# Reordering the TensorE and ScalarE program of a windowed-attention and feed-forward kernel, with a silu built from exp and ln

## The chip, the core and the metric

The kernel runs on one core of a Trainium2 chip. The metric is the device time of one execution in microseconds (us); the figure quoted for a kernel is the median of its runs. Lower is better.

## The reference, cut to what matters

The input is `x`, 2048 tokens of 448 features in bf16. It is normalised once (`xn`, no learned scale), and two branches read `xn`:

```python
# branch A: 16 heads of 28; each token looks at itself and at 7 earlier tokens, every second one
qkv = xn @ wqkv                        # 448 -> 3*448
logits = einsum(q, k[pos - 2*w]) * 28**-0.5     # w = 0..7, masked where pos - 2*w < 0
o = softmax(logits) . v[pos - 2*w]
s = o @ wo                             # 448 -> 448
# branch B: feed-forward
h = gelu(xn @ w1 + b1)                 # 448 -> 1792, tanh approximation
y = h @ w2 + b2                        # 1792 -> 448
g = silu(y)
return x + s * g
```

## The kernel before, in words

The tokens are loaded with the even ones first and the odd ones behind them, so that "every second token" becomes "the token before" and the window is 8 neighbours. They are held as 16 tiles of 128 tokens (index `t`) and as 4 chunks of 512 tokens (index `c`). `xnT` is the normalised input with features on the partitions.

**Jobs.** `qk_job(c, g, which)` makes q or k of one group of four heads for a chunk: 4 matmuls, and a cast by VectorE out of PSUM. `v_job(b)` makes v for one block of 128 keys: 4 matmuls, and a copy by ScalarE. `ffn1_pair(c, m0)` makes two of the 14 slices of the hidden layer: 8 matmuls, then two gelu activations on ScalarE into `hT`. `ffn2_job(t)` makes `y` of one tile: 14 matmuls and an addition by VectorE. `silu_job(t)` makes `g`, as twice silu: one Tanh on ScalarE, one VectorE operation. `wo_job(t)` makes the output of one tile: 4 matmuls, two VectorE operations (`sg` and `o_t`) and a store from SP's queue.

**Units.** Attention is done in 17 units: for chunk `c` and head group `i`, four blocks of 121 queries against 128 keys each; the last block (16) of all four groups is unit 4 of chunk 3. `qk_unit` makes the scores (16 matmuls into two PSUM buffers of pool `psA`), two Exp activations on ScalarE (`E`), and two VectorE multiplications of `E` by a mask. `av_unit` then makes the sums `psD` (4 matmuls) and the products `psO` (16 matmuls), Ln and Exp(-x) on ScalarE for the reciprocal (`ld`, `R`), and a VectorE multiplication into `oT`.

**PSUM.** Pool `psA` has two buffers, shared by `ffn1_pair` and by the two score tiles of a unit: the first scores behind a feed-forward stage need both buffers, and so the last gelu. Pool `psB` has four buffers, shared by all the rest.

**Tables.** Gelu and Tanh are in one table set of ScalarE, Exp and Ln in another; `preload_act_table_set` puts the change between them into the program.

**Order.** PE and ScalarE run in the order in which the program writes their instructions (`manual_schedule`). The instructions of VectorE, GpSimd and SP are ordered by the framework's planner. For every chunk `c` the program runs a stage of seven `ffn1_pair(c, ...)`, between them the silu of the chunk before, the normalisation and transposition (`ln_apply`, `ln_tr`) of the chunk after, and the `wo_job`s that are complete by then; then four units of chunk `c`, each as scores, one `ffn2_job`, up to three projections of the next chunk, `av_unit`. Chunk 3 has five units and no projections left to put between them. After the last unit come a change of table set, four silus and the last five `wo_job`s.

Of the kernel before, what the change touches and what calls it, by code (L numbers as in the profile page):

```python
# [8 lines left out]
F32 = mybir.dt.float32  # L9
BF16 = mybir.dt.bfloat16  # L10
U32 = mybir.dt.uint32
ALU = mybir.AluOpType
ACT = mybir.ActivationFunctionType
ENG = mybir.EngineType

S, D, H, DH, F = 2048, 448, 16, 28, 1792
P = 128
NT = S // P
NC = 4
# [4 lines left out]
QB = 121  # L24
# [9 lines left out]
def kernel(  # L34
# [14 lines left out]
    nc = tc.nc  # L49
# [4 lines left out]
    def dram_rows(par, t0, n):  # L54
        cls, r = divmod(t0 * P, S // 2)
        return par[cls, r:r + n * P, :].rearrange("(t p) d -> p t d", p=P)
# [3 lines left out]
    work = ctx.enter_context(tc.tile_pool(name="work", bufs=2))  # L60
# [11 lines left out]
    y_sb = [big.tile([P, D], F32, name=f"y_{i}") for i in range(4)]  # L72
    g_sb = [big.tile([P, D], BF16, name=f"g_{i}") for i in range(8)]
# [18 lines left out]
    def xt(t):  # L92
        return x_sb[t // 4][:, t % 4, :]
# [55 lines left out]
    def ln_stats(t):  # L149
        st = work.tile([P, 6], F32, name="st", tag="st", bufs=4)  # L150
        nc.vector.bn_stats(out=st[:], in_=xt(t))  # L151
        nc.vector.bn_aggr(out=mv[:, t, :], in_=st[:])

    def ln_rstd(t0, n):
        nc.scalar.activation(lnv[:, t0:t0 + n], mv[:, t0:t0 + n, 1], ACT.Ln, bias=eps_t[:])
        nc.scalar.activation(rstd[:, t0:t0 + n], lnv[:, t0:t0 + n], ACT.Exp, scale=-0.5)  # L156

    def ln_apply(t):
        nc.vector.tensor_scalar(xnb[t % 4][:, 0:D], xt(t), mv[:, t, 0:1], rstd[:, t:t + 1],  # L159
                                op0=ALU.subtract, op1=ALU.mult)  # L160

    def ln_tr(t):
        pT = psB.tile([P, KT, P], BF16, name="pT", tag="B")
        for kt in range(KT):
            nc.tensor.transpose(pT[:, kt, :], xnb[t % 4][:, kt * P:(kt + 1) * P], ident[:])  # L165
        nc.vector.tensor_copy(xnT[:, :, LEAD + t * P:LEAD + (t + 1) * P], pT[:, :, :])  # L166

    def qk_weights(kt):

        src = wqkv[:, kt, 0:32]  # L170
        nc.vector.tensor_copy(wqk[:, kt, :, :],
                              bass.AP(src.tensor, src.offset, [list(src.ap[0]), [DH, 2 * H], [1, 32]]))

    def qk_job(c, g, which):
        ps = psB.tile([P, CH], F32, name="ps_qk", tag="B")
        for kt in range(KT):
            nc.tensor.matmul(ps[:, :], wqk[:, kt, 16 * which + 4 * g:16 * which + 4 * g + 4, :],  # L177
                             xnT[:, kt, LEAD + c * CH:LEAD + (c + 1) * CH],
                             start=(kt == 0), stop=(kt == KT - 1))
        dst = (qT, kT)[which]  # L180
        nc.vector.tensor_copy(dst[:, g, LEAD + c * CH:LEAD + (c + 1) * CH], ps[:, :])  # L181

    def v_job(b):
        ps = psB.tile([P, D], F32, name="ps_v", tag="B")
        o = LEAD + QB * b - 7
        for kt in range(KT):
            nc.tensor.matmul(ps[:, :], xnT[:, kt, o:o + P], wqkv[:, kt, 2 * D:3 * D],  # L187
                             start=(kt == 0), stop=(kt == KT - 1))
        nc.scalar.copy(vw[b][:, :, 0:DH], ps[:, :].rearrange("p (h c) -> p h c", h=H))  # L189

    def ffn1_pair(c, m0):
        ps = psA.tile([P, 2, CH], F32, name="ps_h", tag="A")
        for i in range(2):
            m = m0 + i
            for kt in range(KT):
                nc.tensor.matmul(ps[:, i, :], w1[:, kt, m * P:(m + 1) * P],  # L196
                                 xnT[:, kt, LEAD + c * CH:LEAD + (c + 1) * CH],
                                 start=(kt == 0), stop=(kt == KT - 1))
        for i in range(2):
            m = m0 + i  # L200
            nc.scalar.activation(hT[0][:, m, :], ps[:, i, :], ACT.Gelu_apprx_tanh, bias=b1f[:, m:m + 1])  # L201

    def ffn2_job(t):
        c, tt = divmod(t, 4)
        ps = psB.tile([P, D], F32, name="ps_y", tag="B")
        for m in range(MT):
            nc.tensor.matmul(ps[:, :], hT[0][:, m, tt * P:(tt + 1) * P], w2[:, m, :],  # L207
                             start=(m == 0), stop=(m == MT - 1))
        nc.vector.tensor_tensor(out=y_sb[t % 4][:], in0=ps[:, :], in1=b2bc[:], op=ALU.add)

    def silu_job(t):
        th = work.tile([P, D], BF16, name="th", tag="th", bufs=2)
        nc.scalar.activation(th[:], y_sb[t % 4][:], ACT.Tanh, scale=0.5)  # L213
        nc.vector.scalar_tensor_tensor(out=g_sb[t % 8][:], in0=th[:], scalar=1.0, in1=y_sb[t % 4][:],  # L214
                                       op0=ALU.add, op1=ALU.mult)

    def wo_job(t):
        ps = psB.tile([P, D], F32, name="ps_s", tag="B")
        for g in range(4):
            nc.tensor.matmul(ps[:, :], oT[:, g, t * P:(t + 1) * P], wo[:, g, :],  # L220
                             start=(g == 0), stop=(g == 3))
        sg = work.tile([P, D], BF16, name="sg", tag="sg", bufs=2)
        nc.vector.scalar_tensor_tensor(out=sg[:], in0=ps[:, :], scalar=0.5, in1=g_sb[t % 8][:],  # L223
                                       op0=ALU.mult, op1=ALU.mult)
        o_t = work.tile([P, D], BF16, name="o_t", tag="o_t", bufs=3)
        nc.vector.tensor_tensor(out=o_t[:], in0=xt(t), in1=sg[:], op=ALU.add)
        nc.sync.dma_start(dram_rows(out_par, t, 1)[:, 0, :], o_t[:])
# [45 lines left out]

    SET_EXP, SET_GELU = "natural_log_exp_and_others", "gelu_apprx_tanh_and_others"

    def qkv_jobs(c):
        for g in range(4):
            for which in range(2):
                yield lambda g=g, which=which: qk_job(c, g, which)
        for b in range(4 * c, 4 * c + 4 + (c == 3)):  # L280
            yield lambda b=b: v_job(b)

    def run(it, n):
        for _ in range(n):
            f = next(it, None)
            if f is None:
                return
            f()


    with tc.manual_schedule(engines={ENG.PE, ENG.Activation}):
        nc.scalar.preload_act_table_set(SET_EXP)
        for t in range(4):
            ln_stats(t)
            ln_rstd(t, 1)
            ln_apply(t)
            ln_tr(t)
        for kt in range(KT):
            qk_weights(kt)
        for t in range(4, 8):  # L300
            ln_stats(t)
        ln_rstd(4, 4)
        run(qkv_jobs(0), 99)
        wo_next = 0
        for c in range(NC):

            nc.scalar.preload_act_table_set(SET_GELU)
            done = min(NT, 4 * QB * c // P)
            silu = iter(range(4 * (c - 1), 4 * c)) if c else iter(())
            for k in range(MT // 2):  # L310
                ffn1_pair(c, 2 * k)
                t = next(silu, None)
                if t is not None:
                    silu_job(t)
                if c + 1 < NC and k < 4:
                    ln_apply(4 * (c + 1) + k)
                    ln_tr(4 * (c + 1) + k)
                if k >= 2 and wo_next < done:
                    wo_job(wo_next)
                    wo_next += 1  # L320

            nc.scalar.preload_act_table_set(SET_EXP)
            if c + 2 < NC:
                for t in range(4 * (c + 2), 4 * (c + 3)):
                    ln_stats(t)
                ln_rstd(4 * (c + 2), 4)
            jobs = iter(list(qkv_jobs(c + 1))) if c + 1 < NC else iter(())
            n_units = 4 + (c == 3)
            for i in range(n_units):
                E = qk_unit(c, i)  # L330
                if i < 4:
                    ffn2_job(4 * c + i)
                run(jobs, 3 if i < 3 else 99)
                if i == 4:
                    pass
                av_unit(c, i, E)
        nc.scalar.preload_act_table_set(SET_GELU)
        for t in range(12, 16):
            silu_job(t)
        while wo_next < NT:  # L340
            wo_job(wo_next)
            wo_next += 1


# [1 line left out]
_INS = ['A_x', 'A_wqkv', 'A_wo', 'B_x', 'B_w1', 'B_b1', 'B_w2', 'B_b2']  # L346
# [26 lines left out]
```

## Time and profile before

| what | before |
|---|---|
| median of 3 runs | 201.92 us (201.13 to 202.17) |
| the profiled execution's own time | 203.14 us |
| its span, first to last instruction | 201.3 us |
| mean granted TensorE clock | 0.986 |
| TensorE (PE) busy | 172.6 us, 86% of the span |
| ScalarE (ACT) busy | 117.3 us, 58% |
| VectorE (DVE) busy | 111.8 us, 56% |
| chain that ended last, by engine | PE 73%, ACT 11%, DMA 6%, DVE 6%, issue 2% |

The profiled execution took 203.14 us, of which 201.3 us lie between its first and last instruction. PE's matmuls are pipelined, so the busy time of one contains some of its neighbour's; the chain of work that ended last shows the pace at which they follow one another. Granted clock 1.00 is 2.4 GHz.

### The profile page before, as it was taken

Reading aid. Unit: us, or ns where it says so; the run is one execution under the profiler, and the core shown is the slowest. Engines: PE = TensorE matmul, PEld = TensorE weight load, DVE = VectorE, ACT = ScalarE, POOL = GpSimd, SP = SyncE. Lnnn points to the kernel's source line nnn. Section 1 sums busy time; section 2 is a strip of 40 time slices with the busy share of each in tenths; the row PEclk is TensorE's granted clock in tenths of the full one; section 3 lists DMA queues with packets and bytes.
Section 4 is the critical chain, followed back from the end, with each engine's and each line's share of the span. In section 5 each row is a group of like instructions: output and inputs, shape, how many; then the busy total and the mean of one; then the engine's idle time right before and its main releaser. Section 6 shows DMA issues by size and latency. Waiting matters only on the chain.

```text
span 201.3 us, 3396 instructions
## 1 busy us (share of the span) xinstructions
PE 172.6 (86%) x1384; PEld 84.1 (42%) x1384; DVE 111.8 (56%) x220; ACT 117.3 (58%) x181; POOL 16.0 (8%) x56
## 2 busy tenths in 40 slices
PE   0048999979999999799999998899999997998570
PEld 0032445434455454345454543454444443444230
DVE  1886794009775356087753464377651651665494
ACT  0600057684356895745567965754469857657750
POOL 8966000000000000000000000000000000000000
PEclk9999999999999999999999999999999999999787
DMA  5999900000000001000000002000000010000002
GB/s 186 359 229 276 295 2 3 0 0 0 3 0 3 2 0 46 26 0 0 3 0 3 0 23 68 0 5 0 3 0 0 23 49 23 0 3 2 3 23 91
DMA packets 9743, 8.82 MB, mean 44 GB/s; under 512 B 2592, under 2 KB 8832, under 8 KB 9728
## 3 DMA queue, kind: packets, MB, share of 16 engines
q1 hardware_dynamic: 8704, 7.00, 12.4%
q10 hardware_dynamic: 512, 1.20, 1.6%
q0 software_dynamic: 512, 0.40, 1.0%
q8 instruction: 11, 0.18, 0.4%
q14 instruction: 4, 0.03, 0.0%
HBM read 6.77 MB, written 1.84 MB: 43 GB/s over the span
## 4 chain that ended last, share of the span: by engine, by line
PE 73%; ACT 11%; DMA 6%; DVE 6%; issue 2%; DVEq 0%
PE ps_h L196 23%; PE ps_y L207 16%; PE ps_qk L177 15%; PE ps_v L187 6%; DMA wqkv<-in_A_wqkv_dram 6%; PE ps_s L220 5%; ACT E L246 5%; ACT hT L201 3%; PE psD L257 3%; PE S L242 2%; DVE E L248 2%; PE psO L261 2%; ACT ld L266 1%; PE pT L165 1%; DVE sg L223 1%
## 5 line engine op out<-in xcount | busy, mean ns | idle before, releaser
L196 PE MATMUL ps_h<-xnT,w 128*128 128x512 bf16 x224 | 52.3, 379 | 0.2 <-ACT hT L201 0.2
L207 PE MATMUL ps_y<-w,hT 128*128 128x448 bf16 x224 | 45.2, 353 | 0.0
L201 ACT ACTIVATE hT<-ps_h,b1f 128x512 bf16<-128x512 f32 x56 | 35.4, 684 | 15.6 <-PE ps_h L196 15.5
L177 PE MATMUL ps_qk<-xnT,wqk 128*128 128x512 bf16 x128 | 32.1, 406 | 1.9 <-DVE xnT L166 1.9
L246 ACT ACTIVATE E<-S 128x976 bf16<-128x976 f32 x34 | 31.3, 973 | 0.0
L196 PEld LDWEIGHTS <-w 128*128 128x128 bf16 x224 | 21.3, 98 | 23.9 <-issue 0.5
L207 PEld LDWEIGHTS <-hT 128*128 128x128 bf16 x224 | 20.6, 98 | 19.2
L272 DVE TENSOR_TENSOR oT<-psO,R 128x484 bf16<-128x484 f32 (+1 forms) x17 | 11.2, 659 | 26.4 <-ACT R L267 26.4
L266 ACT ACTIVATE ld<-psD 128x484 f32<-128x484 f32 (+1 forms) x17 | 9.8, 574 | 24.0 <-PE psD L257 24.0
L189 ACT CAST vw<-ps_v 128x448 bf16<-128x448 f32 x17 | 9.0, 532 | 23.0 <-PE ps_v L187 23.0
L177 PEld LDWEIGHTS <-wqk 128*128 128x128 bf16 x128 | 13.1, 103 | 18.7 <-issue 3.8
L165 PE MATMUL pT<-ident,xnb 128*128 128x128 bf16 x64 | 6.7, 242 | 12.0 <-DVE xnb L159 12.0
L248 DVE TENSOR_TENSOR E<-E,mk_gen 128x976 bf16<-128x976 bf16 x18 | 12.0, 669 | 7.4 <-ACT E L246 7.4
L220 PE MATMUL ps_s<-wo,oT 128*128 128x448 bf16 x64 | 15.3, 376 | 0.0
L214 DVE SCALAR_TENSOR_TENSOR g<-th,y 128x448 bf16<-128x448 bf16 x16 | 9.8, 624 | 8.8 <-ACT th L213 8.7
L248 DVE TENSOR_TENSOR E<-E,mk 128x976 bf16<-128x976 bf16 x16 | 10.7, 668 | 7.0 <-ACT E L246 6.8
L187 PE MATMUL ps_v<-wqkv,xnT 128*128 128x448 bf16 x68 | 14.0, 352 | 0.0
L223 DVE SCALAR_TENSOR_TENSOR sg<-ps_s,g 128x448 bf16<-128x448 f32 x16 | 9.9, 622 | 7.0 <-PE ps_s L220 7.0
L159 DVE TENSOR_SCALAR xnb<-x,mv,rstd 128x448 bf16<-128x448 bf16 x16 | 5.7, 389 | 13.5 <-ACT rstd L156 13.5
L181 DVE CAST qT<-ps_qk 128x512 bf16<-128x512 f32 x16 | 11.0, 687 | 2.7 <-PE ps_qk L177 2.7
L181 DVE CAST kT<-ps_qk 128x512 bf16<-128x512 f32 x16 | 11.0, 689 | 2.1 <-PE ps_qk L177 2.0
L151 DVE BATCH_NORM_STATS2 st<-x 128x6 f32<-128x448 bf16 x16 | 9.5, 606 | 4.2 <-DMA x<-in_A_x_dram 4.2
(49 smaller groups left out, 136.2 us busy)
## 6 DMA issues: line engine op xcount, KB each, us to landing
out_dram<-o_t SPq DMA_DIRECT2D x16, 112.0 KB, 1.7
w<-in_B_w_dram SPq DMA_DIRECT2D x1, 1568.0 KB, 15.8
x<-in_A_x_dram SPq DMA_DIRECT2D x3, 448.0 KB, 8.7
w<-in_B_w_dram SPq DMA_DIRECT2D x1, 1344.0 KB, 10.3
wqkv<-in_A_wqkv_dram ACTq DMA_DIRECT2D x3, 336.0 KB, 4.5
x<-in_A_x_dram SPq DMA_DIRECT2D x4, 112.0 KB, 4.2
wo<-in_A_wo_dram POOLq DMA_DIRECT2D x16, 24.5 KB, 6.1
w<-in_B_w_dram SPq DMA_DIRECT2D x1, 224.0 KB, 10.3
```

The lines of the kernel that those rows point to most:

```text
L177: nc.tensor.matmul(ps[:, :], wqk[:, kt, 16 * which + 4 * g:16 * which + 4 * g + 4, :], xnT[:, kt, LEAD + c * CH:LEAD + (c + 1) * CH], star ...
L181: nc.vector.tensor_copy(dst[:, g, LEAD + c * CH:LEAD + (c + 1) * CH], ps[:, :])
L187: nc.tensor.matmul(ps[:, :], xnT[:, kt, o:o + P], wqkv[:, kt, 2 * D:3 * D], start=(kt == 0), stop=(kt == KT - 1))
L196: nc.tensor.matmul(ps[:, i, :], w1[:, kt, m * P:(m + 1) * P], xnT[:, kt, LEAD + c * CH:LEAD + (c + 1) * CH], start=(kt == 0), stop=(kt == ...
L201: nc.scalar.activation(hT[0][:, m, :], ps[:, i, :], ACT.Gelu_apprx_tanh, bias=b1f[:, m:m + 1])
L207: nc.tensor.matmul(ps[:, :], hT[0][:, m, tt * P:(tt + 1) * P], w2[:, m, :], start=(m == 0), stop=(m == MT - 1))
L220: nc.tensor.matmul(ps[:, :], oT[:, g, t * P:(t + 1) * P], wo[:, g, :], start=(g == 0), stop=(g == 3))
L223: nc.vector.scalar_tensor_tensor(out=sg[:], in0=ps[:, :], scalar=0.5, in1=g_sb[t % 8][:], op0=ALU.mult, op1=ALU.mult)
L246: nc.scalar.activation(ev, Sp[p2][:, :, :, 0:QW], ACT.Exp, scale=SCALE)
L248: nc.vector.tensor_tensor(out=ev, in0=ev, in1=mk[:, :, :].unsqueeze(1).to_broadcast((P, 2, 4, QW)), op=ALU.mult)
L266: nc.scalar.activation(ld[:, :, 0:n], psD[:, :, 0:n], ACT.Ln)
L272: nc.vector.tensor_tensor(out=dst, in0=psO[:, :, 0:n], in1=R[:, :, 0:n], op=ALU.mult)
```

## The change

The loop over chunks is written out. In chunks 0 to 2, two projections of the next chunk (q and k of head group 0) stand ahead of the first unit's scores, and those that follow are spread differently. Units 0 and 1 of chunk 3 run right behind chunk 2's four units, ahead of chunk 3's feed-forward stage. The `wo_job`s 3 to 6, which ran in chunk 2's feed-forward stage, run inside those two units; 7 to 10, which ran in chunk 3's feed-forward stage, run ahead of and inside units 2 and 3 of chunk 3. The last two `ffn2_job`s share unit 4. The last four silus are made by `silu_exp_job`: three activations, y / (1 + exp(-y)) as exp(-ln(1 + exp(-y))) times y, through one f32 buffer `e`; so the change of table set ahead of the last silus is gone.

```diff
+    def silu_exp_job(t):
+        e = work.tile([P, D], F32, name="se", tag="se", bufs=1)
+        nc.scalar.activation(e[:], y_sb[t % 4][:], ACT.Exp, scale=-1.0)
+        nc.scalar.activation(e[:], e[:], ACT.Ln, bias=1.0)
+        nc.scalar.activation(e[:], e[:], ACT.Exp, scale=-1.0)
+        nc.vector.scalar_tensor_tensor(out=g_sb[t % 8][:], in0=e[:], scalar=2.0, in1=y_sb[t % 4][:],
+                                       op0=ALU.mult, op1=ALU.mult)
...
-        run(qkv_jobs(0), 99)
-        wo_next = 0
-        for c in range(NC):
...
+        def feed_forward_1(c, wos):
             nc.scalar.preload_act_table_set(SET_GELU)
-            done = min(NT, 4 * QB * c // P)
-            silu = iter(range(4 * (c - 1), 4 * c)) if c else iter(())
             for k in range(MT // 2):
                 ffn1_pair(c, 2 * k)
-                t = next(silu, None)
-                if t is not None:
-                    silu_job(t)
+                if c and k < 4:
+                    silu_job(4 * (c - 1) + k)
                 if c + 1 < NC and k < 4:
                     ln_apply(4 * (c + 1) + k)
                     ln_tr(4 * (c + 1) + k)
-                if k >= 2 and wo_next < done:
-                    wo_job(wo_next)
-                    wo_next += 1
+                if k >= 2 and wos:
+                    wo_job(wos.pop(0))
             nc.scalar.preload_act_table_set(SET_EXP)
...
-            jobs = iter(list(qkv_jobs(c + 1))) if c + 1 < NC else iter(())
-            n_units = 4 + (c == 3)
-            for i in range(n_units):
+        for c in range(2):
+            n = c + 1
+            feed_forward_1(c, [0, 1, 2] if c else [])
+            between = [lambda: q(n, 0), lambda: q(n, 1), lambda: (q(n, 2), qk_job(n, 3, 0)),
+                       lambda: (qk_job(n, 3, 1), vs(4 * n, 4 * n + 1)), lambda: vs(4 * n + 2, 4 * n + 3)]
+            between[0]()
+            for i in range(4):
                 E = qk_unit(c, i)
-                if i < 4:
-                    ffn2_job(4 * c + i)
-                run(jobs, 3 if i < 3 else 99)
-                if i == 4:
-                    pass
+                ffn2_job(4 * c + i)
+                between[i + 1]()
                 av_unit(c, i, E)
-        nc.scalar.preload_act_table_set(SET_GELU)
-        for t in range(12, 16):
-            silu_job(t)
-        while wo_next < NT:
-            wo_job(wo_next)
-            wo_next += 1
+        feed_forward_1(2, [])
+        between = [lambda: q(3, 0), lambda: vs(12, 13), lambda: (vs(14, 15), qk_job(3, 1, 0)),
+                   lambda: (qk_job(3, 1, 1), qk_job(3, 2, 0)), lambda: (qk_job(3, 2, 1), v_job(16))]
+        between[0]()
+        for i in range(4):
+            E = qk_unit(2, i)
+            ffn2_job(8 + i)
+            between[i + 1]()
+            av_unit(2, i, E)
+        E = qk_unit(3, 0)
+        q(3, 3)
+        wo_job(3)
+        av_unit(3, 0, E)
+        E = qk_unit(3, 1)
+        for t in range(4, 7):
+            wo_job(t)
+        av_unit(3, 1, E)
+        feed_forward_1(3, [])
+        wo_job(7)
+        wo_job(8)
+        E = qk_unit(3, 2)
+        ffn2_job(12)
+        wo_job(9)
+        av_unit(3, 2, E)
+        silu_exp_job(12)
+        E = qk_unit(3, 3)
+        ffn2_job(13)
+        wo_job(10)
+        av_unit(3, 3, E)
+        silu_exp_job(13)
+        E = qk_unit(3, 4)
+        ffn2_job(14)
+        ffn2_job(15)
+        av_unit(3, 4, E)
+        silu_exp_job(14)
+        silu_exp_job(15)
+        for t in range(11, 16):
+            wo_job(t)
```

Here `q(c, g)` stands for both `qk_job`s of a group and `vs(...)` for several `v_job`s.

## Rows read from the trace of the kernel before

**Rows 1.** The page, busy time of the engines and granted clock in 40 slices.

```profile
PE 172.6 (86%) x1384; PEld 84.1 (42%) x1384; DVE 111.8 (56%) x220; ACT 117.3 (58%) x181; POOL 16.0 (8%) x56
...
PEclk9999999999999999999999999999999999999787
```

**Rows 2.** The chain that ended last, 41 to 72 us: start, length, engine, tile, line.

```profile
41.95 1.27 ACT hT L201 x2
...
58.84 1.73 PE ps_qk L177 x8
60.56 0.76 PE ps_v L187 x4
61.32 0.32 PE psD L257 x4
61.64 0.21 PE psO L261 x16
61.85 0.33 PE S L242 x16
62.19 2.75 PE ps_y L207 x14
...
69.80 1.73 PE ps_h L196 x8
```

**Rows 3.** The same chain, the feed-forward stages of chunks 2 and 3.

```profile
114.90 0.76 PE ps_s L220 x4
...
125.09 1.27 ACT hT L201 x2
...
155.43 1.89 PE ps_h L196 x8
...
167.28 1.27 ACT hT L201 x2
```

**Rows 4.** The same chain, one unit of chunk 3 without projections.

```profile
172.48 0.40 PE psD L257 x2
...
174.11 1.76 ACT E L246 x2
175.89 0.68 DVE E L248
...
176.61 0.40 PE psD L257 x2
```

**Rows 5.** Busy time in stretches: stretch, length, engines (instructions), granted clock, DMA.

```profile
167.20:186.00 18.80, 16.59 (x217) 8.56 (x217) 9.47 (x15) 13.86 (x19) 0.00 (x0) 1.00 0.02 7
186.00:190.00 4.00, 1.37 (x21) 0.88 (x21) 2.00 (x3) 2.62 (x4) 0.00 (x0) 0.88 0.02 4
190.00:192.50 2.50, 2.50 (x9) 0.98 (x9) 1.44 (x3) 2.44 (x4) 0.00 (x0) 0.51 0.00 0
```

**Rows 6.** Groups by line and shape: busy us, mean ns; idle before and releaser.

```profile
L201 ACT ACTIVATE hT<-ps_h,b1f 128x512 bf16<-128x512 f32 x56 | 35.4, 684 | 15.6 <-PE ps_h L196 15.5
L246 ACT ACTIVATE E<-S 128x976 bf16<-128x976 f32 x34 | 31.3, 973 | 0.0
...
L223 DVE SCALAR_TENSOR_TENSOR sg<-ps_s,g 128x448 bf16<-128x448 f32 x16 | 9.9, 622 | 7.0 <-PE ps_s L220 7.0
...
L267 ACT ACTIVATE R<-ld 128x484 f32<-128x484 f32 x16 | 9.7, 606 | 0.5
L266 ACT ACTIVATE ld<-psD 128x484 f32<-128x484 f32 x16 | 9.2, 576 | 22.6 <-PE psD L257 22.6
...
L322 ACT ACT_TABLE_LOAD x4 | 5.1, 1283 | 0.1
```

**Rows 7.** The chain's pieces on VectorE in the tail, the last one included.

```profile
191.65 0.63 DVE sg L223
...
192.72 0.68 DVE g L214 x2
...
198.01 0.39 DVE o_t L226
```

More of the change, by code (lines that the diff above doesn't have):

```diff
@@ L274 @@
     SET_EXP, SET_GELU = "natural_log_exp_and_others", "gelu_apprx_tanh_and_others"
[L276 to L288, printed above, removed]
     with tc.manual_schedule(engines={ENG.PE, ENG.Activation}):
@@ L302, with q, vs @@
         ln_rstd(4, 4)
-        run(qkv_jobs(0), 99)
-        wo_next = 0
-        for c in range(NC):
+        for g in range(4):
+            for which in range(2):
+                qk_job(0, g, which)
+        for b in range(4):
+            v_job(b)
+        def q(c, g):
+            qk_job(c, g, 0)
+            qk_job(c, g, 1)
+        def vs(*bs):
+            for b in bs:
+                v_job(b)
+        def feed_forward_1(c, wos):
             nc.scalar.preload_act_table_set(SET_GELU)
-            done = min(NT, 4 * QB * c // P)
-            silu = iter(range(4 * (c - 1), 4 * c)) if c else iter(())
             for k in range(MT // 2):
                 ffn1_pair(c, 2 * k)
-                t = next(silu, None)
-                if t is not None:
-                    silu_job(t)
+                if c and k < 4:
+                    silu_job(4 * (c - 1) + k)
                 if c + 1 < NC and k < 4:
```

## The prediction

> **What bounds the kernel now.** I read the page first: PE is busy 86% of the span, no other engine comes near, and the granted clock stands at full until the last three slices [rows 1]. So the question is where PE stands still. The chain that ended last answers it, because it names what PE waits for. It stands still in four kinds of place. (1) Behind each feed-forward stage the first scores need the PSUM buffers that the last two gelus read: 1.27 us, with issue 1.33, at 41.95, 125.09 and 167.28 [rows 2, 3], and likewise at 83.14, four times in all. (2) At the start of chunk 3's feed-forward stage the third pair runs only at 155.43 [rows 3], because gelu waits for the unit before and a table load. (3) Chunk 3's units have no projections between them and go at the pace of a chain over three engines: `psD` at 172.48, Exp for the next unit from 174.11, mask, next `psD` at 176.61 [rows 4]. That is 4.13 us a unit; PE's own work in it is 0.33 (scores) + 2.75 (`ffn2`) + 0.53 (`psD`, `psO`) = 3.61 [rows 2]. The fifth unit has no `ffn2`. (4) After that PE was busy only 1.37 of 4.00 us, the clock fell, and for 2.5 us it was granted 0.51, the 1.2 GHz level [rows 5]. Then comes a tail in which VectorE finishes the outputs; its last operation starts at 198.01 and takes 0.39 [rows 7], 2.9 us ahead of the span's end at 201.3.
>
> PE's pace, from the chain: a `qk_job` 0.865 (1.73 for two), a `v_job` 0.76, an `ffn1_pair` 1.73, an `ffn2_job` 2.75, scores 0.33, products 0.32 + 0.21 = 0.53 [rows 2], a `wo_job` 0.76 [rows 3].
>
> **Projections ahead of the first scores (chunks 0 to 2).** No work is added: 1.73 us of projections move in front, where PE waited 1.33. It saves 1.33 in each chunk if nothing behind becomes late. Late next would be unit 0's products, which need the mask. From the end of the stage: gelu to 1.27, table load 1.28 [rows 6] to 2.6, two small activations (some 0.5) to 3.1, two Exp (1.85, as each 0.973 overlaps the next) to 4.95, mask 0.68 to 5.65. PE gets there at 1.73 + 0.33 + 2.75 + 1.73 = 6.54: 0.9 to spare. Unit 3, with two `v_job`s left instead of three, takes PE 0.33 + 2.75 + 1.52 + 0.53 = 5.13 against the chain's 4.13: 1.0 to spare. So I take the whole saving, 2.66 for chunks 0 and 1; if the cover were gone in every chunk it would be nothing.
>
> **Output products taken out of chunk 2's feed-forward stage.** Four `wo_job`s of 0.76 go: 3.04, all paid again later. ScalarE doesn't become the limit: two gelus 1.27 and a Tanh, about as long as `ld`'s 0.58, overlapping by 0.1 each, are 1.65, and PE has at least 1.73 a pair. The stage ended at 125.07 and now ends at X = 125.07 - 2.66 - 3.04 = 119.37. From here I count from X.
>
> **Chunk 2's units.** PE: 6 `qk_job`s 5.19, 5 `v_job`s 3.80, 4 `ffn2` 11.0, scores 1.32, products 2.12, together 23.43, without a wait by the same test (unit 0's products at 6.33 against a mask at 5.15). The third saving of 1.33 is in this.
>
> **Units 0 and 1 of chunk 3.** Unit 0: scores, two `qk_job`s, one `wo_job` bring PE to 26.25. The chain of three engines starts at the last `psD`, 22.90, takes 4.13 and some 0.12 for a copy of v on ScalarE: second half of `psD` at 27.15, end at 27.55. PE waits 0.77. Unit 1: scores and three `wo_job`s, ready at 30.16; chain at 31.28, end 31.70: it waits 1.0. VectorE has much to do here: in about 4 us two masks, two casts and a product, five operations that I take at a mask's 0.68 each [rows 4], and one or more pairs of `sg` 0.62 [rows 6] and `o_t` 0.39 [rows 7], 4.4 and more. A mask that stands behind a cast or an `sg` comes up to 0.7 late. For two units the bounds are 0 and 1.5; I take 0.5, nearer the low end, since both can also run while ScalarE does its Exp.
>
> **Chunk 3's feed-forward stage.** As before, the third pair waits for gelu: `ld` and `R` of 0.6 each from 31.70, table load 1.28, two gelus 1.27 give 35.52, where PE is ready at 31.70 + 3.46 = 35.16: 0.36. Five more pairs: the stage ends at 44.17. The wait behind it (1.33) is covered by two `wo_job`s of 1.52: 45.69.
>
> **Units 2 to 4 and the new silu.** Unit 2: scores, `ffn2`, `wo_job` bring PE to 49.53; mask ready at 44.17 + 1.33 + 1.28 + 1.85 + 0.68 = 49.31. No wait, end 50.06. `silu_exp_job` replaces one Tanh by three dependent f32 activations on 448 columns. The nearest rows are `ld` 0.576 and `R` 0.606 on 484, and, for an activation with a bias, gelu's 0.684 on 512 [rows 6]; low bound 3 x 0.55, high 3 x 0.69, taken 3 x 0.6 = 1.8. They stand in ScalarE's order ahead of the next unit's Exp, so unit 3's chain takes 4.13 + 1.8 = 5.93: second half of `psD` at 55.4, end 55.94. PE is ready at 50.06 + 0.33 + 2.75 + 0.76 = 53.90, done at 54.43 without the wait: 1.5 lost. Unit 4 has both last `ffn2`s: PE at 55.94 + 0.33 + 5.5 = 61.78, chain 55.4 + 5.93 = 61.34. Hidden. End 62.31.
>
> **The tail.** PE's five `wo_job`s (3.8) end at 66.1, at full clock, since it has no stretch left like 186 to 190 us. Two chains follow. ScalarE: `R` done at 63.4, silu 14 to 65.2, `g` 0.62 to 65.8, silu 15 only then, because `e` has one buffer, to 67.65, `g`, `sg`, `o_t` to 69.35. VectorE, from its first `ps_s` at 63.3: five times 1.01 for `sg` and `o_t`, a product and two `g` at 0.62 each, as `sg`'s is, make 6.9, to 70.2 if nothing overlaps. I take 69.8 between the two. With the 2.9 behind it: X + 72.7. The table load that goes costs nothing either way: it ran beside VectorE's work.
>
> **Sum.** 119.37 + 72.7 + 0.5 (VectorE in units 0 and 1) = 192.6 us span against 201.3: 8.7 us less. By place: four gelu waits 5.3, the units of chunk 3 (before: 21.4 us from 168.6 to 190.0 for 15.3 of PE's work, 6.1 lost; now 0.77 + 1.0 + 1.5) 2.8, the slow clock 1.3, less 0.5 and 0.2. The profiled execution would be 203.14 - 8.7 = 194.4; it stood 1.2 above the median, so the median comes to 201.92 - 8.7 = **193.2 us**.
>
> **The clock, and a rule against the change.** The two early units of chunk 3 and the start of the next stage have PE pausing four times in some 12 us. The row nearest to that is 167.2 to 186.0: PE paused in every unit, 16.59 of 18.80 us busy, and the clock was granted at 1.00 [rows 5]. So I cost the pauses at their length. The Trainium skill, "TensorE: Matmul & The Clock Gate", section "A second HAM failure mode: psum-queue depth-cycling", says that short idle spells between groups of matmuls as PSUM buffers cycle can make the clock swing between its levels, with a loss between the bursts. That stretch of this trace doesn't show it.
>
> **Rivals.** *Tail by order* (0.11): the planner puts both last `g` ahead of the `sg`s on VectorE. Then five pairs of 1.01 start at 68.3 and end at 73.35 instead of 69.8: 196.7 us. Against it: before, VectorE did its first `sg` of the tail at 191.65 and the `g`s behind it [rows 7]. *Masks late* (0.07): casts and `sg` stand ahead of masks in every unit; units with 0.9 to spare hide 0.7, the three without lose 0.7 each: 2.1 more, 195.3. *The fill is given back* (0.05): the casts of the early projections push unit 0's masks beyond the 0.9, and three times 1.33 are lost: 197.2; VectorE's work in that unit leaves room for it only if the masks come last. *The clock falls* (0.06), the one on the other side: PE's pauses in units 0 and 1 bring it to 1.2 GHz, and the matmuls behind take twice as long. Chunk 3's stage alone has 12.1 us of them, so it would be about 205 if the whole stage is slow; from 8.7 us of such matmuls on the change loses. For it: the fall at 186 to 190. Against it: the row above. Better than all I allow (0.01): no VectorE delay and a perfect tail, 191. The forecast itself, 192.0 to 194.6, has 0.70.
>
> **Numbers.** About 0.5%, 1 us, is what a measurement of this kernel can tell from no change. The range 191.2 to 197.2 takes in the forecast and the first three rivals. Of the clock's 0.06 I put 0.04 beyond and 0.02 within 0.5%: faster 0.94, same 0.02, slower 0.04.
>
> **What would show it.** No ScalarE gelu wait ahead of any first scores; X near 119.4; chunk 3's stage starting near X + 32 and ending near X + 44.5; the longest PE pause in unit 3 of chunk 3, some 1.5 us; no slice of the clock under full until PE's end. I'd be wrong by size if PE waits for VectorE's masks in chunks 0 to 2, or if the last output comes more than 5 us behind the last matmul; wrong in kind if the clock falls.

## The result and the profile after

The changed kernel takes 192.53 us (median of 4 runs, 191.62 to 192.78) against 202.04 us for the kernel before (four runs; the 201.92 us of the prediction is the median of the first three): a ratio of 0.9527, 95% interval 0.949 to 0.9564, 9.5 us less by the medians. The forecast was 193.2 us, 8.7 us less.

The page of the kernel after, busy time and granted clock, to be set against [rows 1]:

```profile
PE 167.2 (88%) x1366; PEld 82.3 (43%) x1384; DVE 110.9 (58%) x220; ACT 120.5 (63%) x188; POOL 15.9 (8%) x56
...
PEclk9999999999999999999999999999999999999998
```

The profiled execution has a span of 189.9 us against 201.3, which is 11.4 less and more than the medians show. The chain that ended last says why, at its first and last rows below. Both kernels are the same up to the end of chunk 0's feed-forward stage. That point comes at 39.76 us here, with the first projection of chunk 1, and came at 41.93 before, 0.02 us of issue ahead of the gelu at 41.95 [rows 2]. 2.2 us of the 11.4 therefore belong to this execution's start. From that point to the end of the span it is 201.3 - 41.93 = 159.4 us before and 189.9 - 39.76 = 150.1 after: **9.2 us less**. Below, every kernel is measured from that point, called S.

The chain that ended last, kernel after (start, length, engine, tile, line):

```profile
39.76 1.73 PE ps_qk L177 x8
41.49 0.34 PE S L251 x16
...
117.05 1.73 PE ps_qk L177 x8
118.78 0.33 PE S L251 x16
...
142.55 0.67 DVE E L257
143.22 0.27 DVE qT L181
143.49 0.24 issue
143.74 0.67 DVE E L257
144.45 0.40 PE psD L266 x2
...
146.77 0.53 DVE sg L232
147.31 1.24 DVE E L257 x2
148.58 0.40 PE psD L266 x2
...
161.63 1.51 PE ps_s L229 x8
163.15 0.33 PE S L251 x16
...
169.07 0.59 ACT se L221
169.68 0.58 ACT se L222
170.26 0.88 ACT E L255
...
172.99 0.23 PE psD L266
...
180.27 0.59 ACT R L276
...
184.25 0.61 DVE sg L232
...
185.16 0.12 DVE g L223
...
186.57 0.39 DVE o_t L235
```

No gelu stands ahead of any first scores any more: projections (39.76, 117.05) or output products (161.63) run there, and the scores follow at once; in [rows 2, 3] a gelu of 1.27 us stood there. Chunk 3's early units still go by ScalarE and VectorE (142.55 to 148.58, `psD` to `psD` 4.13 us as in [rows 4]). In unit 3 the chain passes through the activations of the new silu (`se`) and only then reaches Exp.

The stretches of the kernel after that answer to [rows 5] (stretch, length, busy time of PE, PEld, DVE, ACT, POOL, granted clock, DMA):

```profile
167.50:173.50 6.00, 4.76 (x58) 2.48 (x54) 4.36 (x8) 4.50 (x8) 0.00 (x0) 1.00 0.07 22
173.50:179.80 6.30, 6.30 (x69) 3.24 (x66) 3.90 (x7) 4.57 (x8) 0.00 (x0) 1.00 0.05 18
179.80:183.50 3.70, 3.70 (x24) 1.85 (x20) 2.80 (x7) 2.91 (x6) 0.00 (x0) 1.00 0.02 4
```

PE pauses in unit 3 (4.76 of 6.00 us busy), and the clock stays at 1.00 until PE's work is done.

### The profile page after: what moved, and what is told of

Same layout as the page of the kernel before. It is cut to its first block, busy times and chain, and to the rows that moved or that the text cites. A ratio compares the mean times of both kernels' runs of the same rounds, so it can differ in the third digit from the quotient of the medians.

```text
span 189.9 us, 3387 instructions
## 1 busy us (share of the span) xinstructions
PE 167.2 (88%) x1366; PEld 82.3 (43%) x1384; DVE 110.9 (58%) x220; ACT 120.5 (63%) x188; POOL 15.9 (8%) x56
## 4 chain that ended last, share of the span: by engine, by line
PE 77%; DVE 7%; ACT 6%; DMA 6%; issue 3%; DVEq 0%
PE ps_h L196 24%; PE ps_y L207 22%; PE ps_qk L177 14%; PE ps_v L187 7%; DMA wqkv<-in_A_wqkv_dram 6%; PE psD L266 3%; PE S L251 2%; PE ps_s L229 2%; DVE E L257 2%; ACT ld L275 2%; PE psO L270 1%; PE pT L165 1%; DVE sg L232 1%; ACT R L276 1%; ACT E L255 1%
## 5 line engine op out<-in xcount | busy, mean ns | idle before, releaser
L196 PE MATMUL ps_h<-xnT,w 128*128 128x512 bf16 x216 | 50.7, 379 | 0.5
L177 PE MATMUL ps_qk<-xnT,wqk 128*128 128x512 bf16 x118 | 30.8, 395 | 2.4 <-DVE xnT L166 1.9
L214 DVE SCALAR_TENSOR_TENSOR g<-th,y 128x448 bf16<-128x448 bf16 x12 | 7.5, 626 | 12.1 <-ACT th L213 12.1
L229 PE MATMUL ps_s<-wo,oT 128*128 128x448 bf16 x64 | 13.6, 353 | 0.1
L165 PEld LDWEIGHTS <-xnb 128*128 128x128 bf16 x64 | 5.2, 109 | 14.3 <-DVE xnb L159 11.5
```

## The experiments

My account was that the gain is the sum of PE's waits that were covered, each worth its length. The rivals: the covered waits come back later as late masks or casts; the gain is in the clock or in the new silu; VectorE or ScalarE is the limit, so that moved work only moves the wait.

**Only the fills.** The kernel before, with work ahead of the first scores of all four chunks:

```diff
-                if k >= 2 and wo_next < done:
+                if k >= 2 and wo_next < done - 2 * (c == 3):
...
+            run(jobs, 2)
+            if c == 3:
+                for _ in range(2):
+                    wo_job(wo_next)
+                    wo_next += 1
             for i in range(n_units):
                 E = qk_unit(c, i)
...
-                run(jobs, 3 if i < 3 else 99)
+                run(jobs, (2, 3, 3, 99, 99)[i])
```

> The kernel before, with only one part of the change: PE gets work ahead of the first scores of every chunk (two projections in chunks 0 to 2, two output products held back in chunk 3). My account (the gain is the sum of PE's waits that are covered): four waits of 1.33 us go, 5.3 us less than before, 196.7 us; the chunk 3 units still run at 4.13 us each and the clock still falls before the last output products. Rival (the waits come back later as late masks or casts, and the change gains by its reordering of chunk 3): within 1.5 us of before.

Measured: 195.49 us against 201.63 for the kernel before beside it, ratio 0.9705 (0.9669 to 0.9741), 6.1 us less where 5.3 were expected; from S 193.8 - 40.37 = 153.4, 6.0 less. The waits don't come back. They were worth somewhat more than their length. From S to the third pair of chunk 3's stage it is 155.43 - 41.93 = 113.50 before [rows 3] and 149.64 - 40.37 = 109.27 here, so 1.41 for each of three, 0.08 more than the wait. (Most of the 0.08 is in the scores: behind a gelu their last 14 take 0.40 us, as in the chain of the next kernel, and behind projections all 16 take 0.34.) From that pair to the end of the last gelu it is 168.55 - 155.43 = 13.12 before and 11.62 here: the two output products held back go with their whole 1.5 us, since what follows hangs on ScalarE from the last gelu on, and not on PE. These four make 5.7; the other 0.2 of the 6.0 are found with the clock, below.

The chain of this kernel, from which those points are taken:

```profile
40.37 1.73 PE ps_qk L177 x8
...
149.64 1.89 PE ps_h L196 x8
...
159.99 1.27 ACT hT L201 x2
```

**Without the fills of chunks 0 to 2.** The kernel after, with `between[0]()` behind the first scores:

```diff
-            between[0]()
             for i in range(4):
                 E = qk_unit(c, i)
+                if i == 0:
+                    between[0]()
```

(the same for chunk 2).

> The changed kernel, with the two early projections of chunks 0 to 2 put behind the first scores instead of ahead of them; all else stays, the fill of chunk 3 too. My account: three waits of 1.33 us come back, 4.0 us more than the changed kernel, 196.5 us. Rival (given back later): under 1.5 us more, up to 194.

Measured: 196.58 us, ratio 0.975 (0.9718 to 0.9783); from S 194.9 - 40.53 = 154.4, 4.2 more than the kernel after (4.0 expected), again 1.4 for each. In its chain the gelu stands ahead of the scores again:

```profile
40.53 1.27 ACT hT L201 x2
41.84 0.40 PE S L251 x14
```

**Half a fill.** The kernel after with one projection ahead of the scores and one behind:

```diff
-            between[0]()
+            qk_job(n, 0, 0)
             for i in range(4):
                 E = qk_unit(c, i)
+                if i == 0:
+                    qk_job(n, 0, 1)
```

(the same for chunk 2, with `qk_job(3, 0, ...)`).

> The changed kernel with one projection instead of two ahead of the first scores of chunks 0 to 2, the second one behind them: 0.865 us of cover for a wait of 1.33. My account: 0.47 us of each wait comes back, and about 0.1 for starting again, three times: 1.4 to 1.7 us more than the changed kernel, from the same point in the profile and in the median (some 194 us). Rival (any work ahead of the scores does, since what counts is that PE doesn't stand still): no difference.

Measured: 193.94 us, ratio 0.9615 (0.9584 to 0.9646); from S 193.5 - 41.75 = 151.8, 1.6 more than the kernel after, 0.54 for each of three. The projection ahead of the scores runs beside the gelu; the gelu is still what they wait for:

```profile
41.77 1.27 ACT hT L201 x2
...
43.09 0.40 PE S L251 x14
```

So the cover counts by its length, at the two lengths tried (0.865 and 1.73 us); to cover the whole wait, what stands ahead of the scores must be as long as it.

**The changed kernel again**, beside the half fill and the last experiment of this section:

> The changed kernel once more, beside the two that follow. From the first projection ahead of chunk 0's first scores to the end of the span its profile shows 150.1 us (189.9 - 39.76); what lies ahead of that varies from execution to execution by more than a microsecond in kernels that are the same up to there. Expected: 192.0 to 193.0 us, 150.1 us again from that point, whatever the start takes. Rival (the start is shortened by the change): the start is again 2 us shorter than before's 41.9.

Measured: 192.38 us, ratio 0.9532 (0.9507 to 0.9557), span 191.1. From S it is 191.1 - 40.92 = 150.2, the same to 0.1 us, while S itself comes 1.2 us later than in the first profile. The half fill, a changed kernel too, has its S at 41.75. So the start's 2 us are no part of the change.

**Tanh again for the last four silus:**

```diff
-        silu_exp_job(12)
...
-        silu_exp_job(13)
...
-        silu_exp_job(14)
-        silu_exp_job(15)
+        nc.scalar.preload_act_table_set(SET_GELU)
+        for t in range(12, 16):
+            silu_job(t)
         for t in range(11, 16):
             wo_job(t)
```

> The changed kernel with the last four silus made by Tanh again, behind the last unit and a change of table set, as in the kernel before. My account: the pause of some 1.5 us in unit 3 of chunk 3 goes, because no three activations stand ahead of its Exp; the tail behind the last unit grows from 6.1 us (end of R to the end of the last o_t) to the 7.6 us of the kernel before; together nothing, 192.1 to 192.9 us. Rival (the silu from exp and ln is what makes the tail short, and pays): 1.3 us slower or more, 193.8 us and up.

Measured: 192.32 us, ratio 0.9531 (0.95 to 0.9562), where the kernel after took 192.53 and 192.38; from S 190.1 - 40.09 = 150.0. The new silu as the change places it is worth nothing. Its chain shows the two sides of that:

```profile
178.92 0.58 ACT R L276
179.52 1.28 ACT L372
180.81 0.58 ACT th L213
...
186.72 0.39 DVE o_t L235
```

`R` ends at 179.50, 139.4 after S, where the kernel after needs 180.86 - 39.76 = 141.1: 1.7 for unit 3's pause. From the end of `R` to the end of the last `o_t` it is 187.11 - 179.50 = 7.6, where the kernel after needs 186.96 - 180.86 = 6.1: 1.5 given back in the tail, by the table load and four late Tanh; the chain runs through the load and the first Tanh, and what each costs was not tried apart.

This run also tells what the clock was worth. The kernel with only the fills has the same tail, but at a lowered clock. Its chain in the tail:

```profile
182.71 0.58 ACT R L267
...
190.51 0.39 DVE o_t L226
```

Its stretches there:

```profile
177.00:181.60 4.60, 1.75 (x39) 0.94 (x39) 3.00 (x5) 2.93 (x4) 0.00 (x0) 1.00 0.00 0
181.60:184.20 2.60, 2.48 (x25) 1.30 (x25) 0.94 (x3) 2.02 (x3) 0.00 (x0) 0.74 0.03 6
184.20:187.00 2.80, 2.80 (x11) 1.24 (x10) 2.46 (x6) 2.55 (x5) 0.00 (x0) 0.63 0.13 41
```

And those of the kernel with Tanh:

```profile
177.90:180.50 2.60, 2.60 (x32) 1.42 (x32) 1.59 (x3) 2.11 (x3) 0.00 (x0) 1.00 0.02 6
180.50:184.00 3.50, 1.89 (x10) 0.78 (x8) 3.16 (x7) 2.46 (x5) 0.00 (x0) 1.00 0.11 33
```

From the end of `R` to the end of the last `o_t`: 190.90 - 183.29 = 7.6 us at a granted clock of 0.74 and 0.63, 7.6 us at 1.00. In the kernel before, at 0.51 [rows 5], `R` ends at 190.79 and the last `o_t` at 198.40 [rows 7]: 7.6 us again. PE's output products are not what these tails wait for, so the lowered clock cost them nothing.

Ahead of `R` it cost a little in the kernel before, whose clock had already fallen when the second half of the last `psD` ran. The rows of the kernel before are these (a stretch, a piece of the chain, a row of the timeline):

```profile
188.90:189.70 0.80, 0.69 (x18) 0.67 (x17) 0.06 (x1) 0.06 (x1) 0.00 (x0) 0.59 0.00 0
189.01 0.29 PE psD L257
190.21 0.58 ACT L267 ACTIVATE R<-ld 128x448 f32<-128x448 f32 x1
```

And those of the kernel with only the fills:

```profile
181.60:182.20 0.60, 0.48 (x18) 0.42 (x17) 0.06 (x1) 0.07 (x1) 0.00 (x0) 1.00 0.00 0
181.72 0.40 PE psD L257 x2
```

From the start of that half of `psD` to the end of `R` it is 190.79 - 189.01 = 1.78 us at the lowered clock and 183.29 - 181.72 = 1.57 at full: 0.2.

**The silus moved out of Exp's way:**

```diff
         av_unit(3, 2, E)
-        silu_exp_job(12)
         E = qk_unit(3, 3)
...
         av_unit(3, 3, E)
-        silu_exp_job(13)
+        silu_exp_job(12)
         E = qk_unit(3, 4)
+        silu_exp_job(13)
...
-        e = work.tile([P, D], F32, name="se", tag="se", bufs=1)
+        e = work.tile([P, D], F32, name="se", tag="se", bufs=2)
```

> The changed kernel with the silus of tiles 12 and 13 moved: 12 behind unit 3's products (where 13 stood), 13 behind unit 4's Exp on ScalarE, and two buffers for e instead of one. My account: unit 3's pause of 1.5 us was the three activations ahead of its Exp and goes; the second buffer takes up to 0.4 us out of the tail: 190.7 to 191.2 us. Rival (ScalarE or VectorE is the limit of these units, so that the pause moves into unit 4): no gain, 192.3 us or more.

Measured: 191.33 us, ratio 0.9482 (0.9449 to 0.9516); from S 190.0 - 41.46 = 148.5, 1.6 less than the kernel after. It lies just above the 190.7 to 191.2 expected. By the medians it is 1.2 less than 192.53; the intervals overlap a little, and the profile carries the finding: `R` ends 139.4 after S, as early as with Tanh, unit 3's products follow PE's output product at 172.32 without a pause, and unit 4 has room for two silus. Its chain there:

```profile
172.32 0.76 PE ps_s L229 x4
173.08 0.35 PE psD L266 x4
...
175.77 0.58 ACT se L222
176.34 1.75 ACT E L255 x2
178.09 0.47 ACT se L220
```

The second buffer gave 0.1 us in the tail (6.0 from the end of `R` against 6.1), not up to 0.4. Whether the two moved silus could do with one buffer was not tried.

**The work spread anew**, on top of the last version:

```diff
-                if k >= 2 and wos:
+                if k >= (1 if c == 3 else 2) and wos:
...
-        between = [lambda: q(3, 0), lambda: vs(12, 13), lambda: (vs(14, 15), qk_job(3, 1, 0)),
-                   lambda: (qk_job(3, 1, 1), qk_job(3, 2, 0)), lambda: (qk_job(3, 2, 1), v_job(16))]
+        between = [lambda: q(3, 0), lambda: vs(12, 13), lambda: vs(14, 15),
+                   lambda: qk_job(3, 1, 0), lambda: qk_job(3, 1, 1)]
...
         E = qk_unit(3, 0)
-        q(3, 3)
+        q(3, 2)
+        qk_job(3, 3, 0)
         wo_job(3)
...
         E = qk_unit(3, 1)
-        for t in range(4, 7):
-            wo_job(t)
+        qk_job(3, 3, 1)
+        wo_job(4)
+        wo_job(5)
+        v_job(16)
         av_unit(3, 1, E)
-        feed_forward_1(3, [])
+        feed_forward_1(3, [6])
```

> The kernel with the silus moved and two buffers for e (191.3 us), and besides with the projections and output products spread anew: chunk 2's units 2 and 3 keep one projection each, units 0 and 1 of chunk 3 get 3.5 and 3.1 us of work for PE (three projections and an output product; a projection, two output products and v of the last block), and output product 6 stands behind the second pair of chunk 3's feed-forward stage. My account (PE's pauses in those two units, 0.8 to 1.3 us each, come from too little work beside a chain of 4.13 us): 1.0 to 2.0 us less, 189.3 to 190.3 us. Rival (VectorE is the limit there, and masks come later when more casts and output operations stand around them): no gain, 191 us or more.

Measured: 189.07 us, ratio 0.9375 (0.9343 to 0.9407); from S 187.3 - 40.22 = 147.1, 1.5 less than the version it is built on; the median is a little under the 189.3 expected at the least. Some 1.1 of the 1.5 lie ahead of chunk 3's feed-forward stage, so most of the pauses came from too little work. (From X, by the timelines, the stage starts at 150.82 - 118.75 = 32.1 in the version before and at 147.67 - 117.51 = 30.2 here, with one output product of 0.76 fewer ahead of it.) Another 0.3 lie in the stage, which takes 12.4 us there and 12.9 here with the 0.76 inside: that product covers the wait for gelu that the forecast put at 0.36. What is left of the pauses is VectorE's, as the rival had it: in unit 0 of chunk 3 `psO` waits 0.22 us for a cast to free its PSUM buffer. That row of its timeline (start, length, engine, line, instruction, idle time before it and what ended it):

```profile
142.93 0.40 PE L270 MATMUL psO<-E,vw 128*32 128x122 bf16 x16 [0.22 <-DVE kT L181]
```

This is the fastest version of the study, 3.3 us under the changed kernel beside which it ran.

## Why the prediction was right, point by point

| point of the forecast | forecast | measured, kernel after |
|---|---|---|
| from S to chunk 2's stage's end (X) | 119.37 - 41.93 = 77.4 | 117.05 - 39.76 = 77.3 |
| X to `psD`, second half, unit 0 of chunk 3 | 27.15, and up to 0.7 for a late mask | 27.4 |
| the same, unit 1 | 31.28 + 0.5 | 31.5 |
| end of chunk 3's stage | 44.17 + 0.5 | 44.6 |
| unit 3's `psD`, second half | 55.4 + 0.5 | 55.9 |
| end of the last `R` | 63.4 + 0.5 | 63.8 |
| end of the last `o_t` | 69.8 + 0.5 | 69.9 |
| end of the span | 72.7 + 0.5 | 72.9 |

(The 0.5 is the term for VectorE in units 0 and 1.)

**The fills** were the largest term and held: 1.33 forecast, 1.4 measured with the fills put in (the kernel with only the fills) and with them taken out (the kernel without those of chunks 0 to 2), and by the length of the cover. The fourth, taken at 1.33, is 1.5. Together 5.7 instead of 5.3, which is most of the difference between 8.7 and 9.2.

**The early units** held, with their pauses and cause. Fills alone bring 153.4 from S, the kernel with Tanh, which has the early units besides, 150.0: they are worth 3.4, with the output products placed in and around them; the two were not taken apart. The term for VectorE was seen as a cast and an `sg` between masks, 143.22 and 146.77, but it was taken at 0.5 and by the second unit it measured 31.5 - 31.28 = 0.25.

**The new silu** held in unit 3. The forecast had `psD` at 55.4 to 55.9 instead of some 54, and 55.9 was measured; the pause, forecast at 1.5, cost 1.7 by the kernel with Tanh. Its activations took 0.565, 0.576 and 0.577 us, where 0.6 with issue was taken.

**Two statements about places were wrong, and they cancelled.** The list by place gave 1.3 us to the slow clock; the three tails of 7.6 us show that it was worth nothing there, and 0.2 ahead of `R`. And "the table load that goes costs nothing either way: it ran beside VectorE's work" is refuted: with table load and Tanh, VectorE gets its `g`s late, and the tail is 1.5 us longer. The tail had been worked out from `R` on, by ScalarE's and VectorE's durations, so the sum came out right; only the list that explained it gave the tail's gain to the clock. From the end of `R` to the end of the last `o_t` the forecast had 69.8 - 63.4 = 6.4, and 6.1 was measured. The 0.2 that the list takes off at its end has no place named. The units' term of 2.8, less 0.5 for VectorE, was 2.3; measured at the end of `R` it is 142.9 - 141.1 = 1.8. By place, then, the 9.2 us are 5.7 for the fills, 0.2 for the slow clock ahead of `R`, 1.8 for the units and 1.5 for the tail.

**The clock rival** didn't come: PE paused in units 0, 1 and 3 of chunk 3 and the granted clock stayed at full to PE's end. The Trainium skill, "TensorE: Matmul & The Clock Gate", section "A second HAM failure mode: psum-queue depth-cycling", tells of a kernel whose clock swung with short idle spells between groups of matmuls; for the spells of this kernel the trace doesn't agree, with 4.76 of 6.00 us busy in unit 3 at a granted clock of 1.00. The other rivals' times, 195.3 to 197.2, weren't reached. Covered waits were not given back, and the tail went in the order hoped for: `sg`s ahead of the last `g`.

## What to carry to other kernels

When an engine waits at each change of stage for the last reader of a buffer, put independent work of at least the wait's length ahead of the first instruction that needs the buffer; here it counted by its length, as far as the wait goes. In a stage that goes by a chain over several engines, give the engine with spare time as much work as the chain is long, from stages that have too much, and keep side work (here the silu) out of the chain's order on the engine that carries it: the same three activations cost 1.7 us ahead of the next Exp and nothing one unit later. A slow clock or a table load in a tail is worth what the chain that ends the tail waits for: here the slow clock was off that chain and cost nothing behind `R`, and the table load was on it.

## What was not expected of the hardware

The first matmuls of the same program differ from execution to execution. The chain's piece of the 32 projections of chunk 0 in the two profiles of the changed kernel, the first one first:

```profile
15.16 8.59 PE ps_qk L177 x32
```

```profile
14.92 9.99 PE ps_qk L177 x32
```

At the later pace (0.216 each) they would take 6.9 us. The time goes at their beginning, where one follows the other every 0.43 us, twice the later 0.216, and this lasts longer in the second execution, by these stretches, the first execution first (PE's busy time and instructions stand behind the length):

```profile
19.00:21.00 2.00, 2.00 (x11) 0.88 (x9) 2.00 (x5) 0.00 (x0) 0.45 (x2) 1.00 1.11 328
```

```profile
19.00:21.00 2.00, 2.00 (x6) 0.70 (x5) 1.36 (x4) 0.00 (x0) 0.45 (x2) 1.00 1.10 329
```

The granted clock is recorded at 1.00 in both. Over all nine profiles S lies between 39.76 and 41.93 us, though the program up to there is the same. A comparison of two single profiles has to begin behind that point; the span alone would have given this change 11.4 us instead of 9.2. What makes the start vary was not tried.
